# An mLSTM layer with an MLP behind it: the prologue of three units in a hand-written order

## The chip, the cores and the metric

The kernel runs on one core of a Trainium2 chip. A core has a matrix engine (PE, with its weight loads shown as PEld), a vector engine (DVE), an activation engine (ACT), a general engine (POOL) and a queue engine (SP) that here only issues DMAs. ACT has a DMA queue of its own beside SP's. The metric is the device time of one execution in microseconds (us); several runs are summed up by their median.

## What is computed

A recurrent attention (mLSTM) over 4 batches x 8 heads x 768 steps with head dimension 40, then an MLP 320 -> 2048 -> 320 with a SiLU between, over all 3072 tokens:

```python
for t in range(S):
    m_new = np.maximum(f_gate[:, :, t] + m, i_gate[:, :, t])
    f_stab = np.exp(f_gate[:, :, t] + m - m_new)
    i_stab = np.exp(i_gate[:, :, t] - m_new)
    C = f_stab * C + i_stab * einsum('bhd,bhe->bhde', vt, kt)
    n = f_stab * n + i_stab * kt
    y[:, :, t] = sigmoid(o_gate) * (C @ qt) / max(|n . qt|, 1.0)
x = y.transpose(0, 2, 1, 3).reshape(B * S, H * D)
h = x @ w_in
return (h * sigmoid(h)) @ w_out
```

The two weight matrices arrive as 64-bit floats; everything else is 32-bit.

## The kernel before

**Units.** The 768 steps are cut into 6 chunks of 128. One chunk of one batch, with all 8 heads, is a unit; there are 24, numbered chunk by chunk, so units 0 to 3 are the first chunk of the four batches and unit 4 is the second chunk of batch 0. A unit takes these steps: loads (`load_d`: the decay tile D, broadcast from the DRAM scratch LFd to 128 partitions, line 258; `load_qk`, line 270; `load_kvo`, line 281; from unit 4 on `load_q`); `decay` (fd by an exp, line 331; a mask by POOL, line 334; eight exps on ACT, line 344); `misc` (a tanh of the output gate, line 349); `scores` (matmuls ps, line 373, then `weigh`: vw, line 385, and two products of ps and D on DVE, line 392); `values` (matmuls po, line 412, then seven DVE instructions from nq, line 418, to the pad copy, line 434, which make x); `state` (matmuls pu, line 442, and the update of C, line 464 for the first chunk); `xpose` (three transposes px of x on PE, line 475, a rounded copy xh on ACT, line 477, and the rest xl on DVE, line 478).

**Gates.** `gates(lo, hi)` makes the running maximum m, the cumulated log decay LF and the transposed gate aT for a range of steps, by two scans and some element operations on DVE (lines 100 to 135), and writes LF to LFd (lines 120 and 121, the second on ACT's queue). `gates(0, L)` serves the first chunk, `gates(L, S)` the other five. D of a unit can be loaded only after LFd has been written.

**Weights.** The weights are made in 18 parts, in the order c0 i0 o0 i1 o1 i2 o2 i3 o3 c4 i4 o4 and so on: i is 256 columns of the first 256 rows of w_in, c is 1024 columns of its last 64 rows, o is 256 rows of w_out. `wload(n)` issues the next n loads on SP, `wmake(n)` makes the next n parts and issues a load after each. Making a part means turning 64-bit floats into 32-bit ones by bit operations (an abs on ACT, line 178, then lines 179, 180, 183 and 187 on DVE) and splitting each into a rounded copy (ACT, line 192 or 202) and a rest (DVE, line 193 or 203).

**The MLP.** Three units make a step (8 steps). For each of 16 column groups fc, `mm1(fc)` multiplies the step's xh and xl with the split w_in (8 matmuls, line 507), then th (ACT line 511, DVE line 512) and its split gh, gl (ACT line 517, DVE line 518); `mm2(fc)`, two groups later, multiplies with the split w_out (9 matmuls, line 535). mm1 needs xh and xl of all three units of the step. fc 0 and 1 need c0, i0 and o0; fc 2 and 3 need i1 and o1; and so on in pairs.

**Buffers.** A pool of 10 large buffers (`pb`) is shared by the four gate tiles f_t, i_t, m_t, LF, the raw weights, the raw q and k of the first eight units, and xh and xl. D and kvo have three buffers each. PSUM has three banks for `psO` (po and pu of the first three units, then the MLP's outputs), two for `psH` (px of the first three units, ph) and three for `psA` (scores, the gates' transposes, later units).

**What sets the order.** SP's instructions run in the order of the program text (`manual_schedule`, line 70); each waits until what it loads exists and its buffer is free, and all behind it wait too. In `gates(0, L)` DVE's instructions keep their order among themselves as well (line 601). On the other engines, and on DVE otherwise, a planner orders the instructions by their place in the text, when their inputs should be ready, and a small preference for lines 511 to 518; it can put other instructions between those of a fixed order. Lines 599 to 643 are the prologue: the text order of loads, gates, the steps of units 0 to 2, five weight parts and the preparation of unit 3. The main loop (lines 646 to 663) then interleaves the MLP steps with the later units and the remaining weights.

Of the kernel before, what the change touches and what calls it, by code (L numbers as in the profile page):

```python
# [8 lines left out]
F32 = mybir.dt.float32  # L9
# [7 lines left out]
B, H, S, D = 4, 8, 768, 40  # L17
L = 128
# [5 lines left out]
UPS = 3  # L24
# [18 lines left out]
def mlstm_mlp_kernel(  # L43
# [50 lines left out]
    nc.sync.dma_start(bm, bmask)  # L94
    nc.gpsimd.memset(one, 1.0)

    def gates(lo, hi):

        init = NEG if lo == 0 else m_t[:, lo - 1 : lo]
        nc.vector.tensor_tensor_scan(  # L100
            m_t[:, lo:hi], f_t[:, lo:hi], i_t[:, lo:hi], init, op0=ALU.add, op1=ALU.max
        )

        l1 = max(lo, 1)
        eng = nc.vector
        eng.tensor_tensor(
            out=f_t[:, l1:hi], in0=f_t[:, l1:hi], in1=m_t[:, l1 - 1 : hi - 1], op=ALU.add
        )
        eng.tensor_tensor(
            out=f_t[:, l1:hi], in0=f_t[:, l1:hi], in1=m_t[:, l1:hi], op=ALU.subtract  # L110
        )
        nc.vector.tensor_scalar(f_t[:, l1:hi], f_t[:, l1:hi], -120.0, None, op0=ALU.max)
        if lo == 0:
            nc.vector.memset(f_t[:, 0:1], 0.0)
        for c in range(lo // L, hi // L):
            sl = slice(c * L, (c + 1) * L)
            nc.vector.tensor_tensor_scan(
                LF[:, sl], one.broadcast_to([BH, L]), f_t[:, sl], 0.0, op0=ALU.mult, op1=ALU.add
            )
        nc.sync.dma_start(LFd[:, 0:H, lo:hi], LF[:, lo:hi])  # L120
        nc.scalar.dma_start(LFd[:, H, lo:hi], LF[0:B, lo:hi])
        eng.tensor_tensor(
            out=i_t[:, lo:hi], in0=i_t[:, lo:hi], in1=m_t[:, lo:hi], op=ALU.subtract
        )
        eng.tensor_tensor(
            out=i_t[:, lo:hi], in0=i_t[:, lo:hi], in1=LF[:, lo:hi], op=ALU.subtract
        )
        c0, c1 = lo // L, hi // L
        pt = psA.tile([128, 512], F32, tag="a", name=f"pt{lo}")
        for c in range(c0, c1):  # L130
            nc.tensor.transpose(
                pt[:, c * BH : (c + 1) * BH], i_t[:, c * L : (c + 1) * L], ident[:BH, :BH]
            )
        nc.vector.tensor_copy(
            aT[:, c0:c1, :], pt[:, c0 * BH : c1 * BH].rearrange("p (c h) -> p c h", h=BH)
        )
# [6 lines left out]
    class Part:  # L143
# [22 lines left out]
                nc.sync.dma_start(to[K:], src[:, :, w:])  # L166

        def make(self):
            K, nb, n, nm = self.K, self.nb, self.n, self.nm
            full = self.raw  # L170
            if wide:


                low, high = full[:, :, :, 0], full[:, :, :, 1]
                bits = pw.tile([128, WN], U32, tag="wt", name=f"wt{nm}")
                bits = bits[:, : nb * n].rearrange("p (a f) -> p a f", a=nb)
                mag = full = bits.bitcast(F32)
                nc.scalar.activation(mag, high.bitcast(F32), AF.Abs)  # L178
                nc.vector.tensor_scalar(mag, mag, TINY, None, op0=ALU.max)
                nc.vector.tensor_scalar(  # L180
                    bits, bits, 3, 0x3FFFFFF8, op0=ALU.logical_shift_left, op1=ALU.bitwise_and
                )
                nc.vector.scalar_tensor_tensor(
                    out=bits, in0=high, scalar=0xC0000000, in1=bits,
                    op0=ALU.bitwise_and, op1=ALU.bitwise_or,
                )
                nc.vector.scalar_tensor_tensor(
                    out=bits, in0=low, scalar=29, in1=bits,
                    op0=ALU.logical_shift_right, op1=ALU.bitwise_or,
                )  # L190
            if K == 128:
                nc.scalar.copy(self.hi, full)  # L192
                nc.vector.tensor_tensor(
                    out=self.lo, in0=full, in1=self.hi.bitcast(F32), op=ALU.subtract
                )
            else:

                for k in range(2):
                    a, b = slice(k * K, (k + 1) * K), slice((1 - k) * K, (2 - k) * K)
                    cs = slice(k * n, (k + 1) * n)  # L200
                    hi = self.hi[a, :, cs]
                    nc.scalar.copy(hi, full[a])
                    nc.vector.tensor_tensor(
                        out=self.hi[b, :, cs], in0=full[a], in1=hi.bitcast(F32), op=ALU.subtract
                    )
# [42 lines left out]
    class Unit:  # L248
# [26 lines left out]
                nc.sync.dma_start(t.rearrange("p w t -> p (w t)"), qk[n, hf])  # L275
                self.raw.append((t[:, 0, :], t[:, 1, :]))

        def load_kvo(self):
            n = self.n
            t = p3.tile([128, 2 * DM + H * D1], F32, tag="kvo", name=f"kvo{n}")  # L280
            nc.sync.dma_start(t, kvo[n])
            self.kt = t[:, :DM]
            self.vt = t[:, DM : DM + H * D1].rearrange("p (h e) -> p h e", e=D1)
            self.ot = t[:, DM + H * D1 :].rearrange("p (h e) -> p h e", e=D)
# [67 lines left out]
                nc.gpsimd.tensor_tensor(out=self.qt, in0=self.qt, in1=self.lq, op=ALU.mult)  # L352

        def scores(self):
            if self.n not in LIGHT:
                self.half(0)
                self.half(1)
                return

            ps = [self.bank_s(hf) for hf in range(2)]  # L360
            for j in range(HH):
                for hf in range(2):
                    self.score(ps[hf], hf, j)
            for hf in range(2):
                self.weigh(ps[hf], hf)

        def bank_s(self, hf):
            return psA.tile([128, HH, L], F32, tag="a", name=f"ps{self.n}_{hf}")

        def score(self, ps, hf, j):  # L370
# [9 lines left out]

        def weigh(self, ps, hf):
            n = self.n
            if hf == 0 and self.c < NC - 1:
                self.vw = p2.tile([128, H, D1], F32, tag="vw", name=f"vw{n}")
                nc.vector.tensor_tensor(
                    out=self.vw,
                    in0=self.vt,
                    in1=self.Dm[:, :, L - 1].unsqueeze(2).broadcast_to([128, H, D1]),
                    op=ALU.mult,
                )  # L390
            hs = slice(hf * HH, (hf + 1) * HH)
            nc.vector.tensor_tensor(
                out=self.Dm[:, hs, :], in0=ps, in1=self.Dm[:, hs, :], op=ALU.mult
            )

        def values(self):
            n, b, c = self.n, self.b, self.c
            po = bank(n, psO, "o", [128, H, D1], f"po{n}")
            flat = po.rearrange("p h e -> p (h e)")
            first = True  # L400
            if c > 0:
# [9 lines left out]
            for h in range(H):  # L411
                nc.tensor.matmul(  # L412
                    po[:, h, :], self.Dm[:, h, :], self.vt[:, h, :], start=first, stop=(h == H - 1)
                )
                first = False
            den = p2.tile([128, H], F32, tag="den", name=f"den{n}")
            nq = p2.tile([128, H], F32, tag="nq", name=f"nq{n}")
            nc.vector.tensor_scalar(nq, po[:, :, D], 1.0, None, op0=ALU.mult)
# [15 lines left out]
            nc.vector.tensor_copy(xf[:, DM : DM + 64], xf[:, DM - 64 : DM])  # L434

        def state(self):
            n, b, c = self.n, self.b, self.c
            if c == NC - 1:
                return
            pu = bank(n, psO, "o", [128, 3, 3 * D1], f"pu{n}")  # L440
            for g, (h0, nh) in enumerate(GRP):
                nc.tensor.matmul(
                    pu[: nh * D, g, : nh * D1],
                    self.kt[:, h0 * D : (h0 + nh) * D],
                    self.vw[:, h0 : h0 + nh, :].rearrange("p h e -> p (h e)"),
                    start=True,
                    stop=True,
                )
            parts = ((KS, 0, 2, 3), (2 * D, 2, 3, 2))
            if c > 0:  # L450
                for K, g0, g1, nh in parts:
# [144 lines left out]
        prep(n + 1, k)  # L596


    wload(1)
    units[0].load_qk()  # L600
    with tc.manual_schedule(engines={mybir.EngineType.DVE}):
        gates(0, L)
    units[0].load_kvo()
    units[0].load_d()
    prepare(0)
    units[1].load_qk()
    units[1].load_d()
    wload(1)
    units[1].load_kvo()
    wload(2)  # L610
    units[0].scores()
    prepare(1)
    units[2].load_qk()
    gates(L, S)
    units[2].load_d()
    units[1].scores()
    units[2].load_kvo()
    units[0].values()
    wmake(1)
    wload(1)  # L620
    prepare(2)
    steps[0] = Step(0)
    units[0].xpose(steps[0])
    units[0].state()
    wmake(1)
    units[2].scores()
    wmake(1)
    units[1].values()
    units[2].values()
    units[1].xpose(steps[0])  # L630
    units[1].state()
    units[3].load_d()
    units[3].load_qk()
    units[2].state()
    units[3].load_kvo()
    wmake(1)
    units[4].load_d()
    prepare(3)
    units[2].xpose(steps[0])
    units[4].load_qk()  # L640
    wmake(1)
    units[4].load_kvo()
# [89 lines left out]
```

## Time and profile before

| quantity | value |
|---|---|
| median of 3 runs | 533.6 us (531.12 to 535.26) |
| the profiled execution, time | 537.91 us |
| its span, first to last instruction | 536.0 us |
| PE busy | 484.6 us, 90% of the span |
| DVE busy | 353.5 us, 66% |
| ACT busy | 275.9 us, 51% |
| POOL busy | 99.3 us, 19% |
| read from and written to memory | 60.94 MB, 4.04 MB |

Everything below is read from one profiled execution. The profile shows what each engine did and when. "Idle before" is the time in which an engine had nothing running just before an instruction, with what ended it. A busy engine is not always the limit: what matters in a stretch is which engine the others wait for there. The granted clock of the matrix engine is shown as a share of full speed. The share of busy time is an average over the whole span; the change touches only the first part of it, so the views by stage are the ones to look at.

### The profile page before, as it was taken

To read this page: it belongs to the slowest core of one execution; us is meant where nothing else is said; L and a number is where in the kernel's file an instruction comes from. 1 tells how busy PE (TensorE), PEld (TensorE's weight loads), DVE (VectorE), ACT (ScalarE), POOL (GpSimd) and SP (SyncE) were. 2 spreads that over 40 slices of the span, in tenths; PEclk is the share of its full clock that TensorE was granted. 3 is DMA by queue.
4 is the path that set the end of the run, shared out by engine and by line. 5 is a ranking of instruction groups with operands and counts; after the bars stand their busy time and mean duration, and the time that the engine had idled before them with its cause. 6 is when DMAs were issued, how large, how long until landed. Compare 5 with 4: busy or idle time off the path is not lost.

```text
span 536.0 us, 8752 instructions
## 1 busy us (share of the span) xinstructions
PE 484.6 (90%) x3134; PEld 469.5 (88%) x3134; DVE 353.5 (66%) x733; ACT 275.9 (51%) x663; POOL 99.3 (19%) x139
## 2 busy tenths in 40 slices
PE   1476879789999989998999999999998999999996
PEld 1376768789898988998999899999998999999996
DVE  6579999886577687667854767557674655454342
ACT  1554776663645567565552755527465434334333
POOL 0111124240243413333121221222110000000000
PEclk9999999999799999999999999999999999999999
DMA  3998962552384646639243351533372001001001
GB/s 99 297 317 256 272 226 67 171 142 84 103 221 136 170 126 177 189 89 243 79 138 104 102 151 52 163 104 96 101 206 66 28 1 38 2 0 38 2 0 38
DMA packets 52526, 65.55 MB, mean 122 GB/s; under 512 B 3195, under 2 KB 40479, under 8 KB 52483
## 3 DMA queue, kind: packets, MB, share of 16 engines
q1 hardware_dynamic: 48963, 60.95, 40.6%
q10 hardware_dynamic: 3520, 4.04, 2.2%
q8 instruction: 25, 0.41, 0.3%
q14 instruction: 18, 0.15, 0.1%
HBM read 60.94 MB, written 4.04 MB: 121 GB/s over the span
## 4 chain that ended last, share of the span: by engine, by line
PE 48%; DMA 25%; DVE 12%; ACT 6%; issue 3%; POOL 2%; SPq 2%; POOLq 0%; ACTq 0%; DVEq 0%
PE ph L507 20%; PE pout L535 19%; DMA D<-LFd 15%; PE po L412 5%; DMA raw<-in_qk_dram 4%; DMA kvo<-in_kvo_dram 3%; ACT D L344 3%; PE ps L373 2%; PE po L403 2%; DVE th L512 2%; POOL D L334 2%; DVE gl L518 1%; DVE st L319 1%; ACT st L317 1%; DMA lq<-LFd 1%
## 5 line engine op out<-in xcount | busy, mean ns | idle before, releaser
L507 PE MATMUL ph<-xh,wh 128*128 128x384 f32 x384 | 134.8, 351 | 7.8 <-DVE th L512 7.3
L507 PE MATMUL ph<-xl,wh 128*128 128x384 f32 x384 | 131.6, 343 | 0.0
L535 PE MATMUL pout<-woh,gh 128*128 128x320 f32 x384 | 122.4, 322 | 7.0 <-ACT gh L517 6.2
L535 PE MATMUL pout<-wol,gh 128*128 128x320 f32 x384 | 117.9, 309 | 0.0
L512 DVE SCALAR_TENSOR_TENSOR th<-th,ph 128x384 f32<-128x384 f32 x128 | 70.1, 549 | 70.9 <-ACT th L511 70.7
L518 DVE TENSOR_TENSOR gl<-th,gh 128x384 fp32r<-128x384 f32 x128 | 75.2, 590 | 62.3 <-ACT gh L517 60.2
L535 PE MATMUL pout<-woh,gl 128*128 128x320 f32 x384 | 110.7, 313 | 1.4 <-DVE gl L518 1.2
L511 ACT ACTIVATE th<-ph 128x384 f32<-128x384 f32 x128 | 62.0, 485 | 63.1 <-PE ph L507 57.8
L517 ACT CAST gh<-th 128x384 fp32r<-128x384 f32 x128 | 65.0, 510 | 55.5 <-DVE th L512 54.0
L507 PE MATMUL ph<-xh,wl 128*128 128x384 f32 x256 | 87.6, 342 | 0.0
L507 PEld LDWEIGHTS ph<-xh,wh 128*128 128x128 f32 x384 | 73.4, 191 | 10.7 <-DVE th L512 9.4
L535 PEld LDWEIGHTS pout<-woh,gh 128*128 128x128 f32 x384 | 72.9, 190 | 10.0 <-ACT gh L517 8.4
L507 PEld LDWEIGHTS ph<-xl,wh 128*128 128x128 f32 x384 | 73.3, 191 | 0.2 <-issue 0.2
L535 PEld LDWEIGHTS pout<-wol,gh 128*128 128x128 f32 x384 | 72.8, 190 | 0.0
L535 PEld LDWEIGHTS pout<-woh,gl 128*128 128x128 f32 x384 | 69.9, 189 | 2.9 <-DVE gl L518 2.8
L344 ACT ACTIVATE D<-D,aT 128x128 f32<-128x128 f32 x192 | 59.9, 390 | 14.7 <-POOL D L334 14.5
L412 PEld LDWEIGHTS po<-kvo,D 128*128 128x128 f32 x384 | 53.6, 215 | 2.2 <-ACT wh L192 1.1
L412 PE MATMUL po<-kvo,D 128*128 128x41 f32 x384 | 54.7, 299 | 0.8 <-ACT wti L178 0.7
L334 POOL TENSOR_SCALAR_AFFINE_SELECT D<-D 128x512 f32<-128x512 f32 x48 | 35.6, 767 | 101.2 <-ACT fd L331 74.3
L319 DVE TENSOR_TENSOR st<-raw,st 40x512 fp32r<-40x512 f32 x64 | 46.5, 727 | 6.6 <-ACT st L317 5.1
L507 PEld LDWEIGHTS ph<-xh,wl 128*128 128x128 f32 x256 | 48.8, 191 | 0.0
L317 ACT CAST st<-raw 120x512 fp32r<-120x512 f32 x64 | 35.7, 620 | 14.7 <-DMA raw<-in_qk_dram 14.7
(71 smaller groups left out, 500.2 us busy)
## 6 DMA issues: line engine op xcount, KB each, us to landing
raw<-in_qk_dram SPq DMA_DIRECT2D x32, 480.0 KB
D<-LFd SPq DMA_DIRECT2D x24, 512.0 KB
kvo<-in_kvo_dram SPq DMA_DIRECT2D x24, 484.0 KB
wro<-in_w_out_dram SPq DMA_DIRECT2D x8, 640.0 KB
wri<-in_w_in_dram SPq DMA_DIRECT2D x8, 512.0 KB
out_dram<-ob ACTq DMA_DIRECT2D x24, 160.0 KB
qt<-in_qp_dram SPq DMA_DIRECT2D x20, 180.0 KB
lq<-LFd SPq DMA_DIRECT2D x60, 60.0 KB
```

Of the source, the lines that this page charges most:

```text
L317: nc.scalar.copy(t, raw)
L319: nc.vector.tensor_tensor(out=t[r0 : r0 + D, :], in0=raw[r0 : r0 + D, :], in1=t[r0 : r0 + D, :].bitcast(F32), op=ALU.subtract,)
L334: nc.gpsimd.affine_select(out=d, in_=d, compare_op=ALU.is_ge, fill=NEG, base=0, pattern=[[0, HH], [1, L]], channel_multiplier=-1,)
L344: nc.scalar.activation(d[:, h, :], d[:, h, :], AF.Exp, bias=aT[:, c, r + h : r + h + 1])
L373: nc.tensor.matmul(ps[:, j, :], k_[:, cs], q_[:, cs], start=True, stop=True)
L412: nc.tensor.matmul(po[:, h, :], self.Dm[:, h, :], self.vt[:, h, :], start=first, stop=(h == H - 1))
L507: nc.tensor.matmul(ph, w, x, start=(i == 0), stop=(i == len(ops) - 1))
L511: nc.scalar.activation(th, ph, AF.Tanh, scale=0.5)
L512: nc.vector.scalar_tensor_tensor(out=th, in0=th, scalar=1.0, in1=ph, op0=ALU.add, op1=ALU.mult)
L517: nc.scalar.copy(gh, th)
L518: nc.vector.tensor_tensor(out=gl, in0=th, in1=gh.bitcast(F32), op=ALU.subtract)
L535: nc.tensor.matmul(self.po[t], g[:, ts], w[:, fc, :], start=(fc == 0 and i == 0), stop=(last and i == 2),)
```

## The change

The helpers are cut into pieces that can be called alone: a weight part's `make` into `make_a` (abs, clamp, shift), `make_b` (the two bit merges) and `make_c` (the split); `scores` of the first eight units into `score_all` and `weigh_all`; `values` into `value` (PE) and `output` (DVE); `state` into `outer` (PE) and `update`. The instructions in them are the same.

The prologue is then written out for units 0 to 2 in a fixed order on DVE, PE, ACT, POOL and SP. The weight parts in it are c0, i0, o0 and i1. kvo of units 0 and 1 is loaded through ACT's queue at the start; the second write of LFd goes to SP's queue; unit 1's scores use the two `psH` banks; `gates(L, S)` and the preparation of unit 3 come at the end of the fixed order. Behind it five parts count as begun by the time the main loop starts, as before (four and one more), and eight loads have been issued in the text instead of ten.

```diff
+    def gates_out(lo, hi):
+        nc.sync.dma_start(LFd[:, 0:H, lo:hi], LF[:, lo:hi])
+        nc.sync.dma_start(LFd[:, H, lo:hi], LF[0:B, lo:hi])
...
-        nc.sync.dma_start(LFd[:, 0:H, lo:hi], LF[:, lo:hi])
-        nc.scalar.dma_start(LFd[:, H, lo:hi], LF[0:B, lo:hi])
+        gates_out(lo, hi)
...
         def make(self):
+            self.make_a()
+            self.make_b()
+            self.make_c()
...
-        def load_kvo(self):
+        def load_kvo(self, eng=nc.sync):
...
-            nc.sync.dma_start(t, kvo[n])
+            eng.dma_start(t, kvo[n])
...
         def bank_s(self, hf):
+            if self.n == 1:
+                return psH.tile([128, HH, L], F32, tag="h", name=f"ps{self.n}_{hf}")
             return psA.tile([128, HH, L], F32, tag="a", name=f"ps{self.n}_{hf}")
...
         def values(self):
+            self.value()
+            self.output()
...
         def state(self):
+            if self.c < NC - 1:
+                self.outer()
+                self.update()
...
-    wload(1)
-    units[0].load_qk()
-    with tc.manual_schedule(engines={mybir.EngineType.DVE}):
+    E = mybir.EngineType
+    u0, u1, u2, u3 = units[: UPS + 1]
+    c0, i0, o0, i1 = parts[:4]
+    steps[0] = None
+    with tc.manual_schedule(engines={E.DVE, E.PE, E.Activation, E.Pool, E.SP}):
+        wload(1)
+        u0.load_qk()
+        u0.load_kvo(nc.scalar)
+        u1.load_kvo(nc.scalar)
+        wload(1)
         gates(0, L)
-    units[0].load_kvo()
-    units[0].load_d()
-    prepare(0)
-    units[1].load_qk()
-    units[1].load_d()
-    wload(1)
-    units[1].load_kvo()
-    wload(2)
-    units[0].scores()
-    prepare(1)
-    units[2].load_qk()
-    gates(L, S)
-    units[2].load_d()
-    units[1].scores()
-    units[2].load_kvo()
-    units[0].values()
-    wmake(1)
-    wload(1)
-    prepare(2)
-    steps[0] = Step(0)
-    units[0].xpose(steps[0])
-    units[0].state()
-    wmake(1)
-    units[2].scores()
-    wmake(1)
-    units[1].values()
-    units[2].values()
-    units[1].xpose(steps[0])
-    units[1].state()
-    units[3].load_d()
-    units[3].load_qk()
-    units[2].state()
-    units[3].load_kvo()
-    wmake(1)
+        u0.load_d()
+        u1.load_qk()
+        u1.load_d()
+        u2.load_qk()
+        u2.load_d()
+        u2.load_kvo()
+        wload(2)
+        for u in (u0, u1, u2):
+            u.split(0, 0)
+        c0.make_a()
+        c0.make_b()
+        i0.make_a()
+        i0.make_b()
+        u0.misc()
+        c0.make_c()
+        i0.make_c()
+        u0.score_all()
+        u0.decay(0)
+        u0.decay(1)
+        u1.misc()
+        u1.score_all()
+        u1.decay(0)
+        u1.decay(1)
+        u0.weigh_all()
+        o0.make_a()
+        u0.value()
+        u0.outer()
+        u2.misc()
+        u2.decay(0)
+        u2.decay(1)
+        u2.score_all()
+        o0.make_b()
+        u0.output()
+        u1.weigh_all()
+        u0.update()
+        steps[0] = Step(0)
+        u0.xpose(steps[0])
+        u1.value()
+        u1.outer()
+        u2.weigh_all()
+        u2.value()
+        u1.output()
+        u1.xpose(steps[0])
+        o0.make_c()
+        u1.update()
+        u2.output()
+        u2.xpose(steps[0])
+        u2.outer()
+        i1.make_a()
+        i1.make_b()
+        i1.make_c()
+        u2.update()
+        u3.load_d()
+        u3.load_qk()
+        u3.load_kvo()
+        prepare(3)
+        gates(L, S)
+    nmade[0] = 4
+    wload(3)
     units[4].load_d()
-    prepare(3)
-    units[2].xpose(steps[0])
     units[4].load_qk()
     wmake(1)
     units[4].load_kvo()
```

More of the change, by code (lines that the diff above doesn't have):

```diff
@@ L168, in make, with make_a @@
         def make(self):
+            self.make_a()
+            self.make_b()
+            self.make_c()
+        def make_a(self):
             K, nb, n, nm = self.K, self.nb, self.n, self.nm
-            full = self.raw
+            self.full = self.raw
             if wide:
-                low, high = full[:, :, :, 0], full[:, :, :, 1]
+                high = self.raw[:, :, :, 1]
                 bits = pw.tile([128, WN], U32, tag="wt", name=f"wt{nm}")
-                bits = bits[:, : nb * n].rearrange("p (a f) -> p a f", a=nb)
-                mag = full = bits.bitcast(F32)
+                bits = self.bits = bits[:, : nb * n].rearrange("p (a f) -> p a f", a=nb)
+                mag = self.full = bits.bitcast(F32)
                 nc.scalar.activation(mag, high.bitcast(F32), AF.Abs)
@@ L182, in make, with make_b @@
                 )
+        def make_b(self):
+            if wide:
+                low, high, bits = self.raw[:, :, :, 0], self.raw[:, :, :, 1], self.bits
                 nc.vector.scalar_tensor_tensor(
@@ L190, in make, with make_c @@
                 )
+        def make_c(self):
+            K, n, full = self.K, self.n, self.full
             if K == 128:
@@ L354, in scores, with score_all, weigh_all @@
         def scores(self):
-            if self.n not in LIGHT:
+            if self.n in LIGHT:
+                self.score_all()
+                self.weigh_all()
+            else:
                 self.half(0)
                 self.half(1)
-                return
-            ps = [self.bank_s(hf) for hf in range(2)]
+        def score_all(self):
+            self.ps = [self.bank_s(hf) for hf in range(2)]
             for j in range(HH):
                 for hf in range(2):
-                    self.score(ps[hf], hf, j)
+                    self.score(self.ps[hf], hf, j)
+        def weigh_all(self):
             for hf in range(2):
-                self.weigh(ps[hf], hf)
+                self.weigh(self.ps[hf], hf)
         def bank_s(self, hf):
+            if self.n == 1:
+                return psH.tile([128, HH, L], F32, tag="h", name=f"ps{self.n}_{hf}")
             return psA.tile([128, HH, L], F32, tag="a", name=f"ps{self.n}_{hf}")
@@ L382, in weigh @@
             n = self.n
+            hs = slice(hf * HH, (hf + 1) * HH)
             if hf == 0 and self.c < NC - 1:
@@ L390, in weigh @@
                 )
-            hs = slice(hf * HH, (hf + 1) * HH)
             nc.vector.tensor_tensor(
@@ L396, in values, with value @@
         def values(self):
+            self.value()
+            self.output()
+        def value(self):
             n, b, c = self.n, self.b, self.c
-            po = bank(n, psO, "o", [128, H, D1], f"po{n}")
+            po = self.po = bank(n, psO, "o", [128, H, D1], f"po{n}")
             flat = po.rearrange("p h e -> p (h e)")
@@ L415, in values, with output @@
                 first = False
+        def output(self):
+            n, po = self.n, self.po
             den = p2.tile([128, H], F32, tag="den", name=f"den{n}")
@@ L436, in state, with outer @@
         def state(self):
+            if self.c < NC - 1:
+                self.outer()
+                self.update()
+        def outer(self):
             n, b, c = self.n, self.b, self.c
-            if c == NC - 1:
-                return
-            pu = bank(n, psO, "o", [128, 3, 3 * D1], f"pu{n}")
+            pu = self.pu = bank(n, psO, "o", [128, 3, 3 * D1], f"pu{n}")
             for g, (h0, nh) in enumerate(GRP):
@@ L448, in state, with update @@
                 )
+        def update(self):
+            n, b, c, pu = self.n, self.b, self.c, self.pu
             parts = ((KS, 0, 2, 3), (2 * D, 2, 3, 2))
```

## The prediction

> **What bounds the kernel now.** I read the busy time by stage first, then the chain of waits, then the timeline of the first 130 us; the whole change lies there. Columns of the stage view: stretch and length, busy time of PE, PEld, DVE, ACT and POOL with instruction counts, granted TensorE clock, DMA share, GB/s.
>
> ```profile
> 0.00:40.00 40.00, 17.64 (x94) 16.26 (x94) 24.71 (x56) 16.11 (x41) 5.65 (x13) 1.00 0.78 237
> 40.00:62.00 22.00, 16.88 (x75) 14.36 (x74) 21.97 (x52) 13.58 (x34) 3.05 (x4) 1.00 0.93 267
> 62.00:118.00 56.00, 47.98 (x307) 44.23 (x306) 53.20 (x106) 35.64 (x86) 17.72 (x19) 1.00 0.56 167
> 140.00:150.00 10.00, 9.97 (x50) 9.04 (x48) 8.42 (x14) 7.59 (x20) 3.62 (x5) 0.66 0.46 130
> ```
>
> The page gives PE 90% of the span, but not here. Up to 40 us nobody is full: DVE idles 40 - 24.71 = 15.3 us. From 40 to 62 DVE has 0.03 us of idle, and in 62 to 118, while PE runs the first MLP step, DVE is busy 53.2 of 56 us against PE's 48.0. So until the first step ends the scarce engine is DVE: it splits all weights, handles the units and makes th and gl.
>
> The chain of waits (start, length, what) and the first MLP matmuls of any length on PE agree:
>
> ```profile
> 2.27 4.75 DMA wrc<-in_w_in_dram
> ...
> 10.58 1.98 DMA LFd<-LF
> ...
> 14.55 8.56 DMA D<-LFd
> ...
> 118.03 0.47 DVE th L512
> ...
> 118.55 1.68 PE ph L507 x8
> ```
> ```profile
> 62.27 0.67 PE L507 MATMUL ph<-xl,wh 128*128 128x384 f32 x1
> ```
>
> The chain runs through the D loads, then almost wholly on DVE from 39 us on, and only at 118.55 does it pass to PE. The first step begins in earnest at 62.27. The reader should keep two quantities apart: when PE may start the step (the change moves it forward), and how much idle DVE has collected by its end (that decides, as long as DVE is the scarcer).
>
> **The change part by part.** No arithmetic is added or removed; order, queues and two PSUM banks change. So I cost the new order as waits. Prices first: DVE (and ACT) busy time of all parts of a kind, i (8 parts), o (8), c (2), in this order:
>
> ```profile
> 0.00:118.00 118.00, 24.07 (x40) 10.10 (x16) 1.00 0.70 210
> ```
> ```profile
> 0.00:118.00 118.00, 28.55 (x40) 11.91 (x16) 1.00 0.70 210
> ```
> ```profile
> 0.00:118.00 118.00, 7.13 (x12) 3.77 (x6) 1.00 0.70 210
> ```
>
> Per part on DVE: i 24.07/8 = 3.0, o 28.55/8 = 3.6, c 7.13/2 = 3.6 us. I divide them over the new make_a, make_b, make_c as 0.9/1.4/0.7, 1.0/1.7/0.9 and 0.85/1.35/1.4, after the number and size of their instructions. From the timeline (start, us, engine, line):
>
> ```profile
> 3.57 0.41 DVE L100 TENSOR_TENSOR_SCAN m_t<-f_t,i_t 32x128 f32<-32x128 f32 x1 [3.57 <-DMA i_t<-in_ig_dram]
> ...
> 7.08 1.28 ACT L178 ACT_TABLE_LOAD   x1 [7.08 <-DMA wrc<-in_w_in_dram]
> ...
> 15.87 0.47 ACT L349 ACTIVATE kvo<-kvo 128x320 f32<-128x320 f32 x1
> ...
> 19.53 0.21 ACT L331 ACTIVATE fd<-D 120x8 f32<-120x8 f32 x1 [3.19 <-DMA D<-LFd]
> ...
> 20.48 2.44 ACT L344 ACTIVATE D<-D,aT 128x128 f32<-128x128 f32 x8 [0.74 <-POOL D L334]
> ...
> 23.02 0.50 DVE L385 TENSOR_TENSOR vw<-kvo,D 128x328 f32<-128x328 f32 x1 [6.06 <-ACT D L344]
> ...
> 23.55 1.29 DVE L392 TENSOR_TENSOR D<-ps,D 128x512 f32<-128x512 f32 x2
> ...
> 27.75 0.78 ACT L178 ACTIVATE wto<-wro 128x640 f32<-128x640 f32 x1
> ...
> 47.04 0.55 DVE L478 TENSOR_TENSOR xl<-px,xh 128x384 fp32r<-128x384 f32 x1
> ...
> 131.78 0.17 DVE L418 TENSOR_SCALAR nq<-po 128x8 f32<-128x8 f32 x1
> ...
> 133.68 0.20 DVE L434 COPY x<-x 128x64 f32<-128x64 f32 x1
> ```
>
> A unit costs ACT 0.47 (misc) and 0.21 + 0.74 (POOL's first select) + 2.44 = 3.4 (decay); DVE 0.50 + 1.29 = 1.8 (weigh), 2.1 (output, seven chained instructions from 131.78 to 133.88), 0.55 (xl) and about as much for update. An xh copy I take at 0.5, near the tanh of 320 columns. PE, grouped over 24 to 62 us (busy, mean ns):
>
> ```profile
> L412 PE MATMUL po<-kvo,D 128*128 128x41 f32 x63 | 14.7, 410 | 0.7 <-ACT wti L178 0.7
> ...
> L442 PE MATMUL pu<-vw,kvo 128*120 128x123 f32 (+1 forms) x24 | 6.0, 412 | 0.7 <-DVE Cm L464 0.7
> L475 PE MATMUL px<-ident,x 128*128 128x128 f32 x9 | 3.4, 450 | 6.3 <-DVE x L431 5.5 <-DVE x L434 0.8
> ```
>
> Per unit: value 16 x 14.7/63 = 3.7, outer 6 x 6.0/24 = 1.5, xpose 3 x 3.4/9 = 1.1 us.
>
> Loads and gates. kvo of units 0 and 1 goes out on ACT's queue before c0 has been issued, with i0 behind: 2 x 484 KB. c0 landed at 7.0 (2.27 + 4.75). Its delay lies between 0 and 968 KB at 267/0.93 = 287 GB/s = 3.4 us; if both queues are served alike, as many bytes as c0 and its predecessors hold (666 KB) pass first, 2.3 us, and I take that: 9.3. The Trainium skill, "DMA: Bandwidth & Descriptors", section "Issuing engines are not separate DMA queues", says that another issuing engine saves only issue time because all share the same 16 DMA engines; by that rule the delay is real, and if it were wrong c0 would still land at 7.0 and the sum below fall by up to 2.3. No row of this trace shows two loaded queues side by side that early. Gates(0, L) without the instructions that were mixed in are done at 6.3, LF at 5.2 instead of 10.56, so D0 is issued at 5.2 + 1.98 = 7.2 and, at the 8.56 us of the D load above, lands by 15.8, just in time. gates_out now puts its second DMA on SP too, one issue in front of D0, hidden in the 1.98.
>
> Now the fixed orders. ACT: table and abs of c0 to 11.3, abs of i0 12.0. DVE waits 6.3 to 11.3 (5.0), then c0.a 12.1, c0.b 13.5, i0.a 14.4, i0.b 15.8, c0.c 17.2, i0.c 17.9. ACT casts i0 to 16.4, decays u0 to 19.8; DVE waits 1.9; weigh of u0 to 21.6. The next DVE instruction is o0.make_a, whose abs stands on ACT behind u1's tanh and decay: 19.8 + 0.47 + 3.4 + 0.78 = 24.5. DVE waits 2.9. Then o0.a and b 27.2, output of u0 29.3, weigh of u1 31.1. The scores of u1 now lie in both psH banks, so u0's xpose gets its bank only after the first half of that weigh, at 30.5: px 31.6, xh 32.1; DVE, done with u0's update at 31.65, waits 0.45, then xl of u0 32.65 and weigh of u2 34.45. PE meanwhile: value of u1 31.6 to 35.3, outer 36.8, value of u2 40.5, and only then u1's xpose, which is queued behind it: 41.6, xh 42.1. DVE waits 0.85 for po1, ends u1's output at 37.4, then stands 4.7 at xl of u1, with o0.c and all else queued behind it. After it xl 42.65, o0.c 43.55, update 44.1, output of u2 46.2, xpose 47.3, xh 47.8: a wait of 1.6. PE may start the step at 47.8, 14.5 us earlier than at 62.27.
>
> DVE idle until then: 3.6 + 5.0 + 1.9 + 2.9 + 0.45 + 0.85 + 4.7 + 1.6 = 21.0, against 15.3 before. That is the heart of the forecast: the units come sooner, but the filler between their steps is gone, and DVE is **5.7 us behind**. ACT's two new DMA issues and POOL's selects, each in front of the exps that need it, lie in waits already counted.
>
> What is late next: gates(L, S) moves from the dead time at 4 to 17 us to the end of the fixed part, and its DMA stands on SP in front of o1, i2, o2.
>
> ```profile
> 4.23 1.53 DVE L100 TENSOR_TENSOR_SCAN m_t<-f_t,m_t,i_t 32x640 f32<-32x640 f32 x1
> ...
> 5.87 0.81 DVE L106 TENSOR_TENSOR f_t<-f_t,m_t 32x640 f32<-32x640 f32 x1
> ...
> 12.21 1.67 DVE L117 TENSOR_TENSOR_SCAN LF<-one,f_t 32x128 f32<-32x128 f32 x5
> ```
>
> To LF it takes 1.53 + 2 x 0.81 + a clamp under 0.81 + 1.67 = 5.3, in all some 7.2 us (two more of 0.81, a copy). From 48.35 on: i1 3.0, update of u2 0.55, 5.3, two fc's of th and gl in between: LF at 59.6. Two writes in front, landing as for c0, 4.75, then the abs: o1 reaches DVE at about 66. Has DVE work until then? Per fc:
>
> ```profile
> L518 DVE TENSOR_TENSOR gl<-th,gh 128x384 fp32r<-128x384 f32 x13 | 8.5, 658 | 0.1
> ...
> L512 DVE SCALAR_TENSOR_TENSOR th<-th,ph 128x384 f32<-128x384 f32 x13 | 7.0, 542 | 0.6 <-ACT th L511 0.6
> ```
>
> i1, update, gates 7.2, four fc's (all that c0, i0 and i1 allow) at 1.2, and u3's 5.0 make 20.5, which lasts to 68.9. So it is just covered: I put 1 us (bounds 0 and 6.5, below). PE stands from about 55 to 69, which costs nothing while DVE is the bound. Once DVE's backlog is done, PE has less left over than at 118.55, having had slack all the time: between 0 and the 1.68 + one mm2 behind it, about 4 us; I take 2.
>
> Sum: 5.7 + 1.0 - 2.0 = **+4.7 us**. The profiled execution took 537.91 (span 536.0), 4.3 over the median; 10 x (1 - 0.66) = 3.4 of that is the clock at 140 to 150, which is no part of the program. So 542.6 in its terms, 533.6 + 4.7 = **538.3** in the median's.
>
> **The rivals.** A, faster: PE's earlier start counts in full, 533.6 - 14.5 = 519.1. For it: PE ends the chain and is busy 86% of 62 to 118. Against: it needs i2 at 54, and i2 is not issued before LF; and DVE's 53.2 of 56. B, slower: SP is held longer. If DVE runs th, gl and u3 ahead of the gates, LF comes as late as 68.9, o1 at 68.9 + 1 + 4.75 + 0.78 = 75.4, DVE idles 6.5: 544.8, a little less if the 1 us above is part of it. It decides once LF is later than 62.4. C, no difference: PE runs at full rate in the fixed part.
>
> ```profile
> 24.30 2.07 PE L373 MATMUL ps<-raw 40*128 40x128 f32 x8 [1.68 <-DVE D L392]
> ...
> 34.66 1.93 PE L412 MATMUL po<-kvo,D 128*128 128x41 f32 x8
> ```
> ```profile
> 80.85 1.02 PE L412 MATMUL po<-kvo,D 128*128 128x41 f32 x8
> ```
>
> Eight po matmuls take 1.93 cold and 1.02 later. With the latter value, outer and xpose halve: the waits of 0.45 and 0.85 vanish, 4.7 becomes 1.05 and 1.6 becomes 1.05, 5.5 in all: 532.8. Against it: from 24.30 to 36.6 PE has eight groups back to back, and the last is still at 1.93; the same kind of work fills the new prologue. The Trainium skill, "TensorE: Matmul & The Clock Gate", section "What's actually happening", would have the clock rise after some 3.4 us of sustained work, inside u1's value, which is C; the 12 us above do not bear it out, so C's chance is kept small on that ground.
>
> **How the numbers follow.** Forecast 0.42 (own range 533.5 to 543.5), A 0.16, B 0.18, C 0.24 (also for waits that I made too long). The range: from C with c0 undelayed (-2.3) and the credit at 4 (-2) and one wait less, 527.5, to B without the credit, 547. One per cent, about what a measurement of this kernel can tell from no change, is 528.3 to 538.9. Faster: A and a sixth of C, 0.20. Slower: B and half of the forecast, 0.39. Same: the rest, 0.41.
>
> **What would show it.** First MLP matmuls near 48 and a stop of PE after four fc's until about 69; DVE idle before 48 of 21 us, with a long wait of xl on xh; the LFd write of the later chunks at 58 to 60 with o1 behind it; the last wol not earlier than 116. If DVE's idle before 48 is under 14 us, or the weights' last subtraction comes before 110, I am wrong on the fast side; if DVE idles over 5 us between 50 and 75, on the slow one.

## The result, and the profile after

The kernel with the change takes 556.08 us (median; 553.44 to 558.03), the kernel before beside it 534.43 us. The ratio is 1.0423 with an interval of 1.0347 to 1.05: the change makes the kernel slower by about 22 us, 9 us beyond the upper end of the forecast's range (547). Ratios here and below are formed from the fast executions alone, so they are not exactly the quotients of the medians. The profiled execution took 555.17 us with a span of 553.3, against 537.91 and 536.0 before.

The stage view is shown again with two stretches, up to 62 us (where the first MLP step began before) and from there to 140. First the changed kernel, then the kernel before; the columns are those of the prediction.

```profile
0.00:62.00 62.00, 34.45 (x171) 31.58 (x171) 35.99 (x79) 22.76 (x59) 8.47 (x15) 1.00 0.44 128
62.00:140.00 78.00, 54.16 (x310) 49.67 (x310) 67.17 (x135) 42.22 (x96) 22.74 (x19) 0.79 0.79 213
```
```profile
0.00:62.00 62.00, 34.52 (x167) 30.62 (x168) 46.68 (x107) 29.70 (x74) 8.70 (x17) 1.00 0.83 248
62.00:140.00 78.00, 68.68 (x453) 63.91 (x452) 65.04 (x134) 43.96 (x106) 20.64 (x25) 1.00 0.49 144
```

By 62 us PE has been busy equally long in both (34.5 us), but DVE has done 10.7 us less, and memory has moved 128 GB/s in place of 248, that is (248 - 128) x 62 = 7.4 MB less. In the next stretch PE is busy 14.5 us less (68.68 - 54.16), nearly the whole difference of 17.3 between the spans, and memory moves more (213 against 144 GB/s): loads that lay before 62 us now come afterwards.

The timeline of SP's queue in the changed kernel (start, us, queue, line, target and source) says why; below it the weight loads of the kernel before in the same place.

```profile
34.34 0.36 SPq L296 DMA_DIRECT2D kvo<-in_kvo_dram  x1
64.48 0.64 SPq L98 DMA_DIRECT2D LFd<-LF  x1
65.17 0.45 SPq L99 DMA_DIRECT2D LFd<-LF  x1
65.72 0.40 SPq L164 DMA_DIRECT2D wro<-in_w_out_dram  x1
66.22 0.41 SPq L164 DMA_DIRECT2D wri<-in_w_in_dram  x1
66.72 0.42 SPq L164 DMA_DIRECT2D wro<-in_w_out_dram  x1
```
```profile
27.01 0.75 SPq L161 DMA_DIRECT2D wro<-in_w_out_dram  x1
27.87 0.40 SPq L161 DMA_DIRECT2D wri<-in_w_in_dram  x1
29.20 1.26 SPq L161 DMA_DIRECT2D wro<-in_w_out_dram  x1
30.55 1.14 SPq L161 DMA_DIRECT2D wri<-in_w_in_dram  x1
```

After unit 3's kvo at 34.34 SP issues nothing for 30 us. It stands at the write of LF, which the second call of the gates has to produce; o1, i2 and o2 are queued behind it and go out at 65.7 to 66.7, where before o1 and i2 went out at 27.0 and 27.9. The DVE rows of the changed kernel, with the idle time before each and what ended it:

```profile
5.87 0.41 DVE L104 TENSOR_TENSOR_SCAN m_t<-f_t,i_t 32x128 f32<-32x128 f32 x1 [5.87 <-DMA i_t<-in_ig_dram]
...
12.64 0.43 DVE L187 TENSOR_SCALAR wtc<-wtc 128x512 f32<-128x512 f32 x1 [3.85 <-ACT wtc L186]
...
29.00 0.49 DVE L187 TENSOR_SCALAR wto<-wto 128x640 f32<-128x640 f32 x1 [5.38 <-ACT wto L186]
...
45.72 0.56 DVE L512 TENSOR_TENSOR xl<-px,xh 128x384 fp32r<-128x384 f32 x1 [3.67 <-ACT xh L511]
...
50.97 0.56 DVE L512 TENSOR_TENSOR xl<-px,xh 128x384 fp32r<-128x384 f32 x1 [1.34 <-ACT xh L511]
...
71.15 0.49 DVE L187 TENSOR_SCALAR wto<-wto 128x640 f32<-128x640 f32 x1 [3.62 <-ACT wto L186]
...
143.61 0.82 DVE L208 TENSOR_TENSOR wol<-wto,woh 128x640 fp32r<-128x640 f32 x1 [1.01 <-ACT woh L207]
```

The row at 143.61 is the last subtraction of the split weights (wol). In the kernel before it stands here:

```profile
115.77 0.82 DVE L193 TENSOR_TENSOR wol<-wto,woh 128x640 fp32r<-128x640 f32 x1 [0.67 <-ACT woh L192]
```

So the split weights are complete 27.8 us later, although PE begins the first MLP step at 51.25 us (row shown further down) and no longer at 62.27.

### The profile page after: what moved, and what is told of

The parts are those of the page before. It is cut to its first block, busy times and chain, and to the rows that moved or that the text cites. A ratio compares the mean times of both kernels' runs of the same rounds, so it can differ in the third digit from the quotient of the medians.

```text
span 553.3 us, 8746 instructions
## 1 busy us (share of the span) xinstructions
PE 486.9 (88%) x3134; PEld 471.5 (85%) x3134; DVE 355.9 (64%) x733; ACT 276.0 (50%) x663; POOL 103.8 (19%) x139
## 4 chain that ended last, share of the span: by engine, by line
PE 55%; DMA 17%; DVE 13%; issue 7%; ACT 5%; SPq 1%; POOL 1%; ACTq 0%; POOLq 0%; DVEq 0%
PE ph L541 23%; PE pout L569 22%; DMA D<-LFd 8%; PE po L439 4%; DMA kvo<-in_kvo_dram 3%; PE ps L396 2%; ACT D L359 2%; DVE st L334 2%; DMA raw<-in_qk_dram 2%; DVE gl L552 2%; DMA LFd<-LF 2%; PE po L430 2%; DMA lq<-LFd 1%; DVE th L546 1%; PE px L509 1%
## 5 line engine op out<-in xcount | busy, mean ns | idle before, releaser
L569 PE MATMUL pout<-woh,gl 128*128 128x320 f32 x384 | 113.3, 316 | 0.9 <-DVE gl L552 0.7
L551 ACT CAST gh<-th 128x384 fp32r<-128x384 f32 x128 | 65.0, 510 | 57.4 <-DVE th L546 55.6
L569 PEld LDWEIGHTS pout<-woh,gh 128*128 128x128 f32 x384 | 73.1, 191 | 10.7 <-ACT gh L551 10.3
L541 PEld LDWEIGHTS ph<-xl,wh 128*128 128x128 f32 x384 | 74.5, 194 | 0.1
L359 ACT ACTIVATE D<-D,aT 128x128 f32<-128x128 f32 x192 | 60.1, 390 | 15.1 <-POOL D L349 15.1
```

Of the source, the lines that this page charges most:

```text
L359: nc.scalar.activation(d[:, h, :], d[:, h, :], AF.Exp, bias=aT[:, c, r + h : r + h + 1])
L541: nc.tensor.matmul(ph, w, x, start=(i == 0), stop=(i == len(ops) - 1))
L551: nc.scalar.copy(gh, th)
L569: nc.tensor.matmul(self.po[t], g[:, ts], w[:, fc, :], start=(fc == 0 and i == 0), stop=(last and i == 2),)
```

## The experiments

Three theories stood at the start. H: the late second gates hold SP's queue, and the weights come too late. F: the front of the new order (kvo on ACT's queue, which delays the gate inputs and c0) costs the time. C: the lower granted clock of the matrix engine (0.79 in place of 1.00 from 62 to 140 us) costs it. Each result below is a ratio to the kernel before, run beside it.

### Loads ahead of the late gates

```diff
         u3.load_kvo()
+        wload(3)
         prepare(3)
         gates(L, S)
     nmade[0] = 4
-    wload(3)
```

> Only the three loads o1, i2, o2 move on SP's queue in front of the write of LFd for the later chunks. Theory H (held loads): the weights were late because SP stood 30 us behind that write while the DMA engines moved 1 GB/s from 40 to 62 us. Then DMA runs in that stretch, DVE's idle of 9.8 us in 62 to 118 falls to under 4, nothing changes before 50 us, and the time falls by about 8 us to 548 (545 to 551). Theory F (front): the loss is made before 50 us, where DVE had 26 us of idle by 62; then the time stays within 2 us of 556. Theory C (clock): the granted clock of 0.75 in 62 to 118 is the loss; if the gap in PE's work closes, the clock returns to 1 and the time falls by 15 us or more.

Measured: 553.31 us, ratio 1.032 (1.0248 to 1.0392), a gain of 1% that is not clear of the noise (the intervals overlap with the changed kernel's) and less than the 8 us that H expected. On SP's queue o1 and i2 now go out at 35.5 and 36.0, but o2 has to wait for a free large buffer until 55.6, and the write of LF, which is behind it, slips to 71.5; everything that follows is held there. The hold was moved by three loads, not removed.

### The second gates early

```diff
         wload(2)
+        gates(L, S)
         for u in (u0, u1, u2):
...
         prepare(3)
-        gates(L, S)
```

> Only gates(L, S) moves, from the end of the fixed order to in front of the first weight part; its write of LFd goes out behind the loads of units 0 to 2 and i1. Theory H: SP is free early, so the gain of the run before, 8 us, and on top the 7 us of DVE work that now fill dead time at 9 to 13 us, less 3 us by which c0 starts later: 12 us, time 544 (541 to 547), first MLP matmuls at about 54 instead of 51. Theory F: the first MLP matmuls come later, so the time rises by 3 us to 559. Theory C: clock as before the change, time 541 or lower.

Measured: 541.14 us, ratio 1.0124 (1.0081 to 1.0167). Of the 4.23% that the change costs, 2.99 points go with this one move, 16 us. SP's queue and the stage view of this kernel:

```profile
20.42 0.63 SPq L98 DMA_DIRECT2D LFd<-LF  x1
...
35.81 0.43 SPq L164 DMA_DIRECT2D wro<-in_w_out_dram  x1
36.29 0.46 SPq L164 DMA_DIRECT2D wri<-in_w_in_dram  x1
36.85 0.41 SPq L164 DMA_DIRECT2D wro<-in_w_out_dram  x1
```
```profile
0.00:62.00 62.00, 32.63 (x165) 29.53 (x166) 40.24 (x88) 21.04 (x54) 9.28 (x17) 1.00 0.84 230
62.00:140.00 78.00, 63.85 (x404) 58.01 (x403) 69.15 (x140) 49.04 (x118) 23.73 (x23) 0.93 0.49 142
```

The write of LF goes out at 20.42, the loads 30 us sooner than in the changed kernel, and memory moves nearly as much by 62 us as before (230 against 248 GB/s). The first MLP matmul comes later than in the changed kernel (54.66 against 51.25 us), and still the kernel is the faster by far. H had expected 544 us and C 541 or lower; the clock is nearly back as well (0.93), so this run does not part the two.

### The early kvo back on SP's queue

```diff
-        u0.load_kvo(nc.scalar)
-        u1.load_kvo(nc.scalar)
         wload(1)
         gates(0, L)
+        u0.load_kvo()
         u0.load_d()
         u1.load_qk()
         u1.load_d()
+        u1.load_kvo()
```

> Only the loads of kvo of units 0 and 1 go back to SP's queue, behind gates(0, L), as before the change. All theories: i_t lands at 3.6 instead of 5.8, c0 near 7 instead of 10.6, LFd is written in 2 instead of 5.9 us, and the first MLP matmuls come about 4 us earlier, at 47. Theory F: the time falls by 4 us or more, to 552 or lower. Theory H: the later loads are still held, but LF of the later chunks and so o1 come 4 us earlier too: 552. Theory C: no change, 556.

Measured: 557.7 us, ratio 1.0377 (1.0293 to 1.0461). PE begins the first step 2 us sooner, at 49.27, and no gain is clear of the noise (the intervals overlap), where F had expected 552 us or less: with the late gates in place this part of the front is worth little, and F falls. H had expected 552 as well, by 4 us less of the hold; the write of LF goes out only 2.3 us sooner (62.19).

### The second unit's transposition ahead of the third unit's value

```diff
         u2.weigh_all()
-        u2.value()
+        o0.make_c()
         u1.output()
         u1.xpose(steps[0])
-        o0.make_c()
+        u2.value()
```

> In the fixed order only: o0's last piece goes in front of unit 1's output, and unit 2's value behind unit 1's transposes. DVE's wait of 3.7 us at xl of unit 1 shrinks to about 1, but unit 2's output then waits for its value by about 1. By my order of waits the first MLP matmuls come 1.5 to 2.5 us earlier, at 49, and the time falls by as much, to 554. If DVE's waits before 50 us do not count (theory H or C alone), it stays at 556.

Measured: 552.27 us, ratio 1.0299 (1.0218 to 1.038); the intervals overlap with the changed kernel's. PE begins the step at 49.08, and the write of LF goes out at 60.76 and not at 64.48: the shorter order also shortens the hold, so this run alone does not say which of the two any gain comes from.

### Early gates, but the queue held all the same

The kernel with the early gates gets one small DMA where the late gates were, on data that DVE makes late:

```diff
         u3.load_kvo()
+        hold = dr.tile([1, 8], F32, name="hold")
+        nc.sync.dma_start(hold, Cm[2][0:1, 0, 0:8])
         prepare(3)
```

> The kernel with the early second gates (541.14 us) plus one small DMA on SP in the place where the late gates stood, which writes eight numbers of the third unit's state to DRAM and so holds the queue until that unit's update on DVE, at about 61 us (in the late kernel the queue was held to 64.48 us). Nothing else is added; the gates' own DVE work, their buffers and their write stay early. Theory H (it is the held queue of loads that costs): o1, i2 and o2 are issued at 61 to 63 us and not at 36, DVE stands more than 5 us longer before the last wol piece, and the time goes back to 549 to 556. Rival D (it is the gates' 7.2 us of DVE work and the four buffers that they keep, which in the late place fill no dead time; the queue's hold is covered): the time stays at 540 to 544 although the loads are late. In between, 545 to 548, both have a share.

Measured: 551.07 us, ratio 1.0313 (1.0247 to 1.0378).

```profile
59.26 0.22 SPq L701 DMA_DIRECT2D hold<-Cm  x1
59.54 0.39 SPq L164 DMA_DIRECT2D wro<-in_w_out_dram  x1
```
```profile
0.00:62.00 62.00, 33.55 (x170) 30.73 (x171) 37.90 (x83) 20.17 (x54) 7.18 (x15) 1.00 0.48 133
62.00:140.00 78.00, 58.89 (x342) 55.19 (x342) 68.32 (x137) 48.95 (x114) 22.96 (x22) 0.78 0.76 217
```

The gates' work is early here and their buffers are free; only SP stands, until 59.26. That alone brings back 1.89 points of the 2.99 (10 us) and the picture of the changed kernel: 133 GB/s by 62 us, 0.78 of the clock behind it. The held queue is therefore the larger part of what the late gates cost. It ends 5 us sooner than in the changed kernel, so the remaining 1.1 points are not all the gates' own work and buffers; those were not separated. Whether some of it acts through the clock, which falls with the hold, this run does not say.

### Both mended orders, and the waits filled

The first kernel has early gates and the transposition's new order. The second has, beside these, kvo on SP's queue (the first unit's behind its D, not ahead of it as above) and i1's making cut up:

```diff
         u1.output()
+        i1.make_a()
         u1.xpose(steps[0])
+        i1.make_b()
         u2.value()
...
         u2.outer()
-        i1.make_a()
-        i1.make_b()
         i1.make_c()
```

> Both mended orders in one kernel: the second gates behind the two weight loads, and o0's last part and the second unit's output and transposition ahead of the third unit's value on PE. If the two gains add (14.9 us and 3.8 us, taken from 556.08), 537.4 us; the wait of DVE for the second unit's transposition falls from 5.89 us to about 2, and the first MLP matmul comes at about 52 and not 54.66. If the transposition only gained by letting the late gates and loads start sooner, the time stays at 540 to 541.

Measured: 542.17 us, ratio 1.0162 (1.0104 to 1.022). The gains do not add: once the gates are early, the transposition's order is worth nothing, though PE begins the step at 53.08 and not at 54.66.

> As the kernel with both mended orders, with kvo of the first two units on SP's queue behind D (so that the gate input i_t lands sooner) and with i1's making put into the second unit's waits on DVE (its first half between output and transposition, its second behind the transposition). If idle DVE before the MLP is what is left of the difference, each microsecond of the wait that is filled counts: i_t's landing 2 us, i1's 2.6 us of DVE work in place of waits, so 3 to 5 us below the kernel with both mended orders, 532 to 535, level with before. If the loads are the bound by then, no gain over that kernel.

Measured: 535.29 us, ratio 1.0008 (0.9966 to 1.005), level with the kernel before, 6.9 us under the kernel just told of, which ran beside it. PE begins the first step only at 59.32 us, 6 us later than there.

### i1's making alone

The kernel with the early gates and, of the edits above, only the cut-up i1:

> The kernel with the early second gates (541.14 us) with one edit more: the first half of i1's making between the second unit's output and its transposition, the second half behind that transposition. kvo stays on ACT's queue and the third unit's value stays ahead of the transposition. The working tiles of the weights are three and are handed out in order, so with i1's making at the end of the hand-laid stretch no later weight can be worked on in DVE's waits of 43 to 54 us. Theory I (that is what held the kernel with filled waits back before): nearly the whole of its gain comes from this edit, 535 to 538 us, with pieces of o1 on DVE before 50 us. Rival K (the earlier kvo order, 2.5 us at the front, gave it): 540 to 542.

Measured: 536.98 us, ratio 1.0036 (0.9997 to 1.0075); the early gates alone had 1.0124, so 0.88 points or 4.7 us come from moving i1. What happens in the wait for the second unit's transposition is seen on DVE. With i1 at the end of the order (the kernel with early gates):

```profile
42.92 0.19 DVE L463 COPY x<-x 128x64 f32<-128x64 f32 x1
49.01 0.56 DVE L512 TENSOR_TENSOR xl<-px,xh 128x384 fp32r<-128x384 f32 x1 [5.89 <-ACT xh L511]
...
55.21 0.43 DVE L187 TENSOR_SCALAR wti<-wti 128x512 f32<-128x512 f32 x1
```

With i1 early:

```profile
43.43 0.20 DVE L463 COPY x<-x 128x64 f32<-128x64 f32 x1
43.54 0.42 DVE L187 TENSOR_SCALAR wti<-wti 128x512 f32<-128x512 f32 x1
43.99 0.43 DVE L188 TENSOR_SCALAR wti<-wti 128x512 uint32<-128x512 uint32 x1
44.33 0.49 DVE L187 TENSOR_SCALAR wto<-wto 128x640 f32<-128x640 f32 x1
44.85 0.49 DVE L188 TENSOR_SCALAR wto<-wto 128x640 uint32<-128x640 uint32 x1
45.38 0.83 DVE L195 SCALAR_TENSOR_TENSOR wto<-wro,wto 128x640 uint32<-128x640 uint32 x1
46.24 0.82 DVE L199 SCALAR_TENSOR_TENSOR wto<-wro,wto 128x640 uint32<-128x640 uint32 x1
```

Of the 5.89 us of waiting 1.6 are left (0.79 in front of the wol at 47.86 and 0.83 in front of xl at 49.51). Two instructions of i1 were moved there, and o1's four came after them by themselves: o1 is made behind the hand-written stretch, and the planner takes it forward as soon as i1 is out of its way. Why o1 did not come forward before is argued, not shown: the working tiles of the weights (bits) are taken to be handed out in the order of the parts, so that o1 gets none before i1. The rows fit this, but nothing was tried that frees o1 from i1 and leaves i1 where it was.

### o0 ahead of the second unit

The kernel with filled waits, with `u0.weigh_all()` and `o0.make_a()` moved ahead of `u1.misc()`, `u1.score_all()` and u1's decays:

> The kernel with filled waits (535.29 us), with o0's first half ahead of the second unit's scores and decays, so that its absolute value on ACT is done before the second unit's exps: DVE's wait of 2.36 us for it at 27.9 goes, and o0's 1.4 us of work move into it. If idle DVE before the last wol piece is still the price, 533 us; if PE or the loads are the bound, no change (534.5 to 536).

Measured: 535.86 us, ratio 1.0008 (0.997 to 1.0046): no change. The wait was not one for ACT's order, as the expectation took it to be. ACT now stands for o0 as well, because its load lands only then:

```profile
27.02 0.77 ACT L186 ACTIVATE wto<-wro 128x640 f32<-128x640 f32 x1 [3.47 <-DMA wro<-in_w_out_dram]
```

### The filled order with late gates

```diff
         wload(2)
-        gates(L, S)
...
         prepare(3)
+        gates(L, S)
```

> The kernel with filled waits (535.29 us) with the second gates put back where the change has them, behind the preparation of the fourth unit. Theory H (the late gates hold SP's queue, so that nothing is there to fill the waits with): the loads of o1 and later weights are issued from about 62 us again and the time is 548 to 556, so that early gates are the condition for every other gain. Rival I (i1 at the end of the hand-laid order is the whole cause, the gates' place none): 535 to 540.

Measured: 548.67 us, ratio 1.0262 (1.018 to 1.0343), against 1.0008 with early gates: the late place costs 2.5 points (13.6 us) here too. Its queue stands until the gates are done, as in the changed kernel:

```profile
56.98 0.64 SPq L98 DMA_DIRECT2D LFd<-LF  x1
...
58.21 0.40 SPq L164 DMA_DIRECT2D wro<-in_w_out_dram  x1
```

### All in one table

The columns come from each kernel's stage view and its timelines: DVE's busy time and the memory rate up to 62 us, PE's busy time from 62 to 140, the start of the first row of MLP matmuls (in the kernel before a single one stood ahead of it, at 57.11), the start of the last wol, DVE's idle time up to there, and the ratio. The idle time is the start of the last wol less DVE's busy time up to it. For the kernel before and the changed one the stretch behind 62 us reads (length, DVE's busy time, granted clock, DMA share, GB/s):

```profile
62.00:115.77 53.77, 51.65 (x103) 1.00 0.56 169
```
```profile
62.00:143.61 81.61, 69.77 (x137) 0.77 0.76 206
```

| kernel | DVE to 62 | GB/s to 62 | PE 62 to 140 | first mm1 | last wol | DVE idle to last wol | ratio |
|---|---|---|---|---|---|---|---|
| before | 46.68 | 248 | 68.68 | 62.27 | 115.77 | 17.4 | 1 |
| filled waits | 48.40 | 234 | 70.73 | 59.32 | 123.24 | 17.8 | 1.0008 |
| early gates, i1 early | 45.88 | 228 | 70.42 | 60.73 | 119.04 | 19.5 | 1.0036 |
| early gates | 40.24 | 230 | 63.85 | 54.66 | 130.15 | 25.9 | 1.0124 |
| filled, late gates | 40.61 | 140 | 56.65 | 48.80 | 143.74 | 34.3 | 1.0262 |
| early gates, held queue | 37.90 | 133 | 58.89 | 54.90 | 135.82 | 30.9 | 1.0313 |
| changed | 35.99 | 128 | 54.16 | 51.25 | 143.61 | 37.9 | 1.0423 |

The time follows how much of its work DVE has got through by 62 us together with whether the loads have been made by then. The two add up in DVE's idle time to the last wol: in all eleven other kernels, those outside the table too, what it has above the kernel before agrees with the difference of the profiled spans within 6 us. By and large the time runs against the start of the MLP: where PE begins the step sooner, DVE has less of its own work behind it. None of the kernels beats the one before.

Theory C is answered in part. The held queue alone brings the low clock with it (0.78), so the clock is no cause of its own here, and it is not the whole: 0.79 stands beside both 1.0262 and 1.0423, and 0.93 beside both 1.0036 and 1.0124. How much of the cost of late loads passes through it was not tried.

## Why the prediction was wrong

**What held.** DVE was named as the scarce engine until the first step ends, and PE's earlier start as worth nothing by itself. The table bears that out, and with it rival A (519.1 us, the earlier start in full) falls. The fixed order did put DVE behind, though by more than the forecast's 5.7 us (21.0 us idle against 15.3): the changed kernel's waits up to 51.5 us sum to 23.5 us over the DVE rows, those of the kernel before to 15.1, so 8.4. The long wait of xl for the second unit was there (3.67 us; 4.7 forecast), and the last one too (1.34; 1.6).

**Details of the front that were off.** The gate input i_t landed at 5.87 us and not at 3.57, since the first kvo went out on ACT's queue ahead of it; c0 came later as well (its DVE work begins at 12.64, forecast 11.3); the write of LF took 5.87 us where the forecast took 1.98 from the kernel before; and the wait for o0 was 5.38 us against 2.9, ended by the load's landing and not by ACT's order. Together they moved the first matmul from the forecast 47.8 to 51.25. The kernel with kvo back on SP gained 2 us of that and no time. ACT's first row that needs c0, in the changed kernel and in that one:

```profile
10.65 1.28 ACT L186 ACT_TABLE_LOAD   x1 [10.65 <-DMA wrc<-in_w_in_dram]
```
```profile
6.46 1.28 ACT L186 ACT_TABLE_LOAD   x1 [6.46 <-DMA wrc<-in_w_in_dram]
```

Two loads on ACT's queue delayed one on SP's by 4.2 us, 3.6 against the kernel before (7.08); the forecast had 2.3. This agrees with the rule of the Trainium skill, "DMA: Bandwidth & Descriptors", section "Issuing engines are not separate DMA queues", which the forecast weighed: another issuing engine saves only the time of issuing.

**The step that failed** is "what is late next": the late gates, "just covered: I put 1 us (bounds 0 and 6.5, below)". The place was right and the price was not: the early gates gain 16 us, and the held queue alone takes 10 of them back. The forecast followed the held queue up to the arrival of o1 and asked only whether DVE has work until then. That part came out some 5 us later than forecast: LF went out at 64.48 (59.6 forecast), o1 reached DVE at 71.15 (66), and DVE idled 4.8 us between 51.5 and 75 (the 3.62 shown above, 0.86 and 0.36) on top of the fixed order's waits, where 1 was forecast. But o1 was only the first of the loads behind the write. With nothing issued on SP's queue from 34.7 to 64.5 us, 7.4 MB less had been moved by 62 us, 24 us of transfers even at 310 GB/s, the highest rate of the changed kernel's stage view in 10 us steps:

```profile
70.00:80.00 10.00, 7.18 (x32) 7.18 (x33) 8.62 (x17) 5.61 (x14) 2.09 (x2) 0.50 1.02 310
```

These came on top of the loads that belong to the time after 62, and the weights were finished late, the last wol by 27.8 us. The kernel with the held queue alone shows that this is the larger share of what the late gates cost. In the forecast's own measure, DVE's idle time, the changed kernel has 20.4 us more up to the last wol than the kernel before: 10.7 up to 62 us (26.0 against 15.3), where the forecast had 5.7, and 9.7 behind it (11.8 against 2.1), where it had 1.0.

**A second term was missing.** The forecast treated the fixed order as one row of waits and did not ask which work outside it could have filled them. With i1 at its end, the wait of 5.89 us stayed empty in the kernel with early gates; moving i1 is worth 4.7 us once the loads are there. Late gates and i1 together are 3.87 of the 4.23 points; the 0.36 left cannot be told from zero.

**The credit** of 2 us for PE's slack was near: 20.4 us more of idle DVE made 17.3 us between the profiled spans, 3.1 less. The last wol itself is later by more than the idle time, 27.8 us, because 7.4 us more of DVE's other work (105.76 us busy up to it against 98.33) lies ahead of it.

**The forecast's rivals.** B was the right mechanism (the queue held longer; it decides once LF is later than 62.4 us, and it was), but it too priced only the wait for o1: 6.5 us for what cost 10 by the hold alone and 13 to 16 by the place of the gates. The forecast's C, the matrix engine at full rate in the fixed part, did not happen: 16 po matmuls still take 3.47 and 3.56 us.

```profile
36.45 3.47 PE L439 MATMUL po<-kvo,D 128*128 128x41 f32 x16
39.72 1.43 PE L474 MATMUL pu<-vw,kvo 128*120 128x123 f32 x6
40.94 3.56 PE L439 MATMUL po<-kvo,D 128*128 128x41 f32 x16
44.29 0.88 PE L509 MATMUL px<-ident,x 128*128 128x128 f32 x3
...
51.25 0.67 PE L541 MATMUL ph<-xh,wh 128*128 128x384 f32 x1
...
55.27 0.52 PE L541 MATMUL ph<-xl,wh 128*128 128x384 f32 x1
55.59 0.37 PE L541 MATMUL ph<-xh,wl 128*128 128x384 f32 x1
55.80 0.34 PE L541 MATMUL ph<-xh,wh 128*128 128x384 f32 x1
```

From 36.45 to 45.17 the groups follow one another without a gap, 8.7 us, and the rate does not rise; it does so 4.3 us into the MLP's long matmuls, from 0.52 to 0.34 us. The rise within some 3.4 us of sustained work that the Trainium skill states ("TensorE: Matmul & The Clock Gate", section "What's actually happening") does not show for the small matmuls of the prologue, while it comes near for the long ones.

**The sign named beforehand** was the right one: DVE idling over 5 us between 50 and 75 would mean too low a forecast. It idled 1.34 us at 50.97 and the 4.8 of the rows after it, 6.2 in all. It is met narrowly: the 1.34 is the last wait of the fixed order, which the forecast had placed before 48 us.

## What to carry to other kernels

When what a queue waits for is moved to a later place, everything behind it in the queue moves too: count what cannot be issued until it is done, in bytes, and the time that memory needs to make it up, not only when the first transfer behind it arrives. When an order is written out by hand, look at its waits as room for work from outside and ask which piece at its end (a shared tile, a place in the order) keeps that work out. An earlier start of the engine that ends the chain says nothing while another engine, here DVE, carries the work that has to be finished.

## What the runs showed of the hardware that was not expected

A write of LF of 16 KB took 1.98 us in the kernel before, where it was issued at 10.58, and 5.87 us in the changed one, issued at 7.71 amid the first loads; with kvo back on SP's queue it still took 4.49, issued at 5.66. What it waits for is not shown.

The granted clock was 1.00 up to 62 us in all seven kernels of the table, although the prologue's po matmuls of the changed kernel took 217 ns each (3.47 us for 16) and those at 80.85 us in the kernel before 128 ns (1.02 us for 8). From 62 to 140 us it was 0.78 to 0.79 in the three kernels with the late loads, where PE often stood, and 0.93 to 1.00 in the other four. In that stretch the ph matmuls of the changed kernel took 382 to 404 ns on average against 353 to 363 in the kernel before, while PE had nothing running for 23.8 us (78 - 54.16). The low clock goes with the waits; whether it added to them was not tried.
